# A transformer block on one core: the beginning and the first stacks by halves, row maxima of 512 columns into a scratch tile

## The chip, the cores and the metric

The kernel runs on one core of one Trainium2 chip. The metric is the device time of one execution in microseconds (us), lower is better. The engines are named as the profile names them: PE (TensorE matmul), PEld (its weight loads), DVE (VectorE), ACT (ScalarE), POOL (GpSimd), SP (SyncE, which here only issues DMAs).

## The reference

One pre-norm transformer block in fp32 over T = 2048 tokens of D = 512 (attention that is causal within segments, with a memory between them, then a gated feed-forward part of 1376 columns):

```python
q, k, v = (x @ wq), (x @ wk), (x @ wv)          # 32 heads of 16, 4 segments of 512 tokens
for s in range(4):
    logits = qs @ ks^T * scale + mask           # causal within the segment
    a_dot = softmax(logits) @ vs
    a_mem = phi(qs) @ M / (phi(qs) @ z + 1e-6)  # memory of the segments before
    o = g * a_mem + (1 - g) * a_dot             # g = sigmoid(beta), by head
    M += phi(ks)^T @ vs;  z += sum(phi(ks))
h  = x + A(layernorm(x)) @ wo
h2 = h + (gelu(y @ w_gate) * (y @ w_up)) @ w_down,   y = layernorm(h)
```

## The kernel before

Most products are made from a high and a low part of each operand (`split_weight`, `split_psum`: ACT writes the high part, DVE or POOL subtracts it to get the low one), and three passes: high by high, low by high, high by low. Buffers are 35 rows of SBUF of 512 columns (`row`), 18 slots of two such halves (`slot`), five stacks each for q and k (`stq`, `stk`), and the 8 banks of PSUM (`bank`). A stack holds q or k of some heads, with high, low and high parts taking turns over the partitions; three DMAs (SP, a few on ACT's queue) put each stack together from a slot (`qkv`, L1131 and L1137).

Every operation on every engine is first recorded (`S.op`), and then emitted by `run(order)` in the order of a table of numbers, `ORDER`. The instructions of an engine stand in that order, and a wait is set where an instruction needs another's result or buffer. A buffer is taken from the pool when its operation comes up in the table. So the table sets all of the sequence and the choice of buffers.

The work of the first segment is this. `ln1_first` fetches four tiles of 128 tokens of x, makes their layer norm in two pairs (statistics on DVE L935, first row of a pair normalised on DVE L958, the second on ACT L962), transposes them on PE (L967) and splits them (L972 high, L974 low). Rows of wq, wk and wv are fetched in between (L698, L715) and split (L699 high on ACT, L704 low on POOL, L707 low on DVE). `project_first` (L1026) makes the first q and k for 256 tokens at a time, `vproj` (L1066) v, `qkv` splits q and k (L1118, L1120) and moves them into stacks.

`pass_a` (L1261) computes scores for the row maxima alone: for each of two heads on two partition halves (`a`) and four blocks of 128 tokens (`i`) a product of 128(i+1) columns. One VectorE instruction (L1271) adds the mask, takes the minimum of the negated sum into one column of `nm`, and has to write its elementwise result somewhere, though nobody reads it. For 512 columns (i = 3) that goes back into the bank, for fewer into the tile `aside`, at offsets 0 and 384 in turn (`turns`). `pass_b` (L1319 to L1347) makes the scores again, transposed, with the maxima in them, then exponentials (L1325) and products with v. `sides` (L574) is a small copy from DVE, `tock`, between two groups of products that use both halves of PE.

The feed-forward part follows (L1612, L1780, L1679), and the last results are sums on DVE (L1683) of rows that POOL has added (L1818) to what was put into DRAM earlier (`y_dram`, fetched again at L1817), then outputs (L1687, L1821).

Of the kernel before, what the change touches and what calls it, by code (L numbers as in the profile page):

```python
# [7 lines left out]
F32 = mybir.dt.float32  # L8
# [506 lines left out]
def infini_geglu(ctx: ExitStack, tc: tile.TileContext, x, wq, wk, wv, wo, beta,  # L515
# [8 lines left out]
    def sb(name, shape, dt=F32):  # L524
        return p0.tile(shape, dt, name=name)
# [1401 lines left out]
```

## Time and profile before

| what | value |
|---|---|
| three runs | 724.71, 725.15 (median), 726.09 us |
| the profiled execution's own time | 727.73 us |
| its span | 726.0 us |
| granted TensorE clock, mean | 0.999 |

A row of the timeline has start (us from the start of the span), duration in us, engine, line, operation, output <- input, how many, and in brackets how long the engine had been idle before, and what released it. A row of the table of stretches has the stretch, its length, and the busy time of PE, PEld, DVE, ACT and POOL with their instructions, then PE's granted clock, the DMA engines' busy share and GB/s. In a list of groups stand busy us and the mean ns of one. SPq and ACTq are the queues that issue DMAs.

### The profile page before, as it was taken

How to read it: one execution, taken by the hardware profiler on the slowest of the kernel's cores; microseconds unless marked ns; L12 is line 12 of the kernel's file. 1: busy time of each engine (PE TensorE's matmuls, PEld its weight loads, DVE VectorE, ACT ScalarE, POOL GpSimd, SP SyncE). 2: the span in 40 equal slices, each digit the busy share in tenths (PEclk: the TensorE clock that was granted, in tenths of full speed). 3: DMA queues.
4: the chain of work that ended last, by engine and by line, in shares of the span. 5: the costliest groups of instructions: out<-in, count | busy, mean ns of one | idle time of the engine just before them, and what ended most of it. 6: DMA issues, size and time to landing. Idle time of an engine off the chain costs nothing. (4 is left out here: it accounts for less than half of the span.)

```text
span 726.0 us, 19146 instructions
## 1 busy us (share of the span) xinstructions
PE 709.3 (98%) x6372; PEld 571.4 (79%) x6372; DVE 628.3 (87%) x1992; ACT 529.9 (73%) x1130; POOL 552.8 (76%) x840
## 2 busy tenths in 40 slices
PE   7999999999999999999999999999999999999997
PEld 6888877767878877876867778888888778888885
DVE  6898989978888889999977686889999998789996
ACT  6889888798777877969677577778876866656331
POOL 6454668498846646868897999999999968599936
PEclk9999999999999999999999999999999999999999
DMA  7755557656676776787668465768573047877757
GB/s 261 188 153 170 147 152 185 186 171 188 188 190 171 207 215 190 212 235 213 176 206 266 149 186 184 240 185 256 163 227 124 16 132 215 273 253 242 249 125 252
DMA packets 102646, 140.49 MB, mean 194 GB/s; under 512 B 18468, under 2 KB 40916, under 8 KB 102548
## 3 DMA queue, kind: packets, MB, share of 16 engines
q1 hardware_dynamic: 102388, 139.02, 65.1%
q8 instruction: 50, 0.82, 0.5%
q14 instruction: 48, 0.39, 0.2%
q10 hardware_dynamic: 160, 0.26, 0.2%
HBM read 73.81 MB, written 39.29 MB: 156 GB/s over the span
## 5 line engine op out<-in xcount | busy, mean ns | idle before, releaser
L1325 ACT ACTIVATE row<-bank 128x512 f32<-128x512 f32 x320 | 172.2, 605 | 36.5 <-PE bank L1319 33.8
L1333 POOL TENSOR_SCALAR_AFFINE_SELECT row<-row 128x256 f32<-128x256 f32 (+1 forms) x320 | 109.1, 369 | 75.1 <-ACT row L1325 74.2
L1271 DVE CUSTOM_DVE_ANT_0 aside<-bank,amask 128x256 f32<-128x256 f32 (+2 forms) x384 | 140.6, 418 | 14.4 <-PE bank L1261 4.8
L1005 PE MATMUL bank<-slot,slot 64*128 64x512 f32 x720 | 109.8, 401 | 0.4 <-DVE tock L574 0.4
L1271 DVE CUSTOM_DVE_ANT_0 bank<-bank,amask 128x512 f32<-128x512 f32 x128 | 86.2, 710 | 7.4 <-PE bank L1261 6.9
L1261 PE MATMUL bank<-stk,stq 64*128 64x128 f32 (+3 forms) x512 | 78.7, 327 | 2.2 <-DVE tock L574 1.2
L1005 PEld LDWEIGHTS bank<-slot,slot 64*128 64x128 f32 x720 | 74.7, 185 | 6.5 <-DVE tock L574 0.6
L1319 PE MATMUL bank<-stq,stk 64*128 64x256 f32 (+3 forms) x512 | 78.0, 331 | 0.6 <-DVE nm L1271 0.2
L1347 PE MATMUL bank<-row,vaug 128*32 128x512 f32 (+3 forms) x1024 | 76.6, 435 | 0.9 <-ACT row L1325 0.3
L1791 DVE TENSOR_TENSOR row<-row,bank 128x512 f32<-128x512 f32 x110 | 71.9, 677 | 4.1 <-PE bank L1780 3.1
L1612 PE MATMUL bank<-slot,slot 128*128 128x512 f32 (+1 forms) x282 | 74.3, 391 | 0.0
L1612 PE MATMUL bank<-slot,stk 128*128 128x512 f32 (+1 forms) x249 | 65.9, 390 | 0.1
L1261 PEld LDWEIGHTS bank<-stk,stq 64*128 64x128 f32 x512 | 55.4, 185 | 12.0 <-issue 2.9
L1319 PEld LDWEIGHTS bank<-stq,stk 64*128 64x128 f32 x512 | 54.0, 185 | 11.9 <-DVE nm L1271 3.6
L1612 PEld LDWEIGHTS bank<-slot,slot 128*128 128x128 f32 (+1 forms) x282 | 51.8, 185 | 12.8 <-DVE row L1461 0.4
L1347 PEld LDWEIGHTS bank<-row,vaug 128*32 128x32 f32 x1024 | 31.1, 109 | 34.9 <-issue 32.0
L1612 PEld LDWEIGHTS bank<-slot,stk 128*128 128x128 f32 (+1 forms) x249 | 46.3, 186 | 10.7 <-DVE row L1637 0.5
L1612 PE MATMUL bank<-slot,stq 128*128 128x512 f32 (+1 forms) x195 | 51.5, 390 | 0.0
L1780 PE MATMUL bank<-slot,half 128*128 128x512 f32 x186 | 50.2, 389 | 0.0
L1054 PE MATMUL bank<-slot,slot 64*128 64x256 f32 x672 | 49.9, 284 | 0.2 <-DVE mb L1186 0.2
L1271 DVE DVE_READ_ACCUMULATOR2_ANT nm<- 128x1 f32 x512 | 49.8, 97 | 0.0
L1619 ACT ACTIVATE vaug<-bank 128x512 f32<-128x512 f32 (+1 forms) x66 | 38.7, 594 | 13.2 <-PE bank L1612 12.8
(244 smaller groups left out, 1782.1 us busy)
## 6 DMA issues: line engine op xcount, KB each, us to landing
stq<-slot SPq DMA_DIRECT2D x96, 128.0 KB
stk<-slot SPq DMA_DIRECT2D x94, 128.0 KB
row<-x SPq DMA_DIRECT2D x32, 256.0 KB
pv_dram<-row SPq DMA_DIRECT2D x32, 256.0 KB
row<-r_dram SPq DMA_DIRECT2D x28, 256.0 KB
wd_dram<-half SPq DMA_DIRECT2D x28, 256.0 KB
half<-wd_dram SPq DMA_DIRECT2D x28, 256.0 KB
row<-wu SPq DMA_DIRECT2D x20, 256.0 KB
```

What stands on the lines that cost most here:

```text
L1005: return nc.tensor.matmul(pm[i].t, w[i].t[rows_of(r), wi, dc * P:(dc + 1) * P], XT[s][dc].t[rows_of(r), xi, :], start=(dc, wi, xi, ph) == ...
L1054: return nc.tensor.matmul(pms[n].t[:, 256 * t:256 * t + 256], XT[s][dc].t[rows_of(r), xi, t0:t0 + P], whl[wi].t[rows_of(r), dc // 2, 256 * ...
L1261: nc.tensor.matmul(sa.t[:, c0:c0 + w], sq.t[own, p, i * P:(i + 1) * P], sk.t[own, p, 0:w], start=True, stop=True, tile_position=(64 * a, 0 ...
L1271: nc.vector.tensor_tensor_reduce(out=(sa.t[:, c0:c0 + w] if i > 2 else aside[:, turns[0]:turns[0] + w]), in0=sa.t[:, c0:c0 + w], in1=amask ...
L1319: nc.tensor.matmul(sc.t[:, c0:c0 + D - q0], sk.t[own, p, q0:q0 + P], sq.t[own, p, q0:D], start=True, stop=True, tile_position=(64 * a, 0), ...
L1325: act(w, prio, lambda sc=sc, e=e: nc.scalar.activation(e.t[:, :w], sc.t[:, :w], AF.Exp), [sc, vtab], [e])
L1333: nc.gpsimd.affine_select(v, v, pattern=pat + [[1, P]], compare_op=OP.is_ge, fill=0.0, base=0, channel_multiplier=-1)
L1347: nc.tensor.matmul(pv.t[32 * n:32 * n + 32, kb * P:D], va.t[:, 136 * kb + 17 * j:136 * kb + 17 * j + 32], e.t[:, lo:lo + D - kb * P], star ...
L1612: nc.tensor.matmul(dst.t[:w], v.t[:, wi, c0 + j * w:c0 + (j + 1) * w], b[bk][j].t[:, xi, :], start=first and j == 0 and n == 0, stop=j == ...
L1619: act(D, prio, lambda: nc.scalar.activation(c.t[:w], src.t[:w], AF.Copy), [src], [c])
L1780: nc.tensor.matmul(dst[u].t, ws[a].t[0][:, wi, P * u:P * u + P], h[bk].t[:, xi], start=first and m == 0, stop=m == 2, skip_group_check=True)
L1791: dve(D, prio, lambda u=u, acc=acc: nc.vector.tensor_tensor(acc.t, acc.t, src[u].t, op=OP.add), [src[u]], [acc])
```

## The change

`ln1_first` halves the normalisation of the second row by columns (ACT 0:256, DVE 256:512) and transposes by pairs of column blocks. In `project_first` each of the three passes is an operation of its own. The first stacks (unit `U` = 0, `Q` = 0) are moved by halves of 256 tokens, and the products of 256 columns in `pass_a` need only the first halves (`EARLY`). The maxima of 512 columns write to `aside` too, which grows from 768 to 960 columns, with offsets 0 and 448 in turn. `ORDER` has other numbers throughout. The number of matmuls stays at 5428. Lines of the changed kernel are some 1 to 22 higher: L1026 becomes L1042, L1131 and L1137 become L1154, L1261 L1283, L1271 L1293, L1683 L1705, L1817 L1839, L1687 L1709, L1821 L1843.

```diff
-    aside = sb("aside", [P, 6 * P])
+    aside = sb("aside", [P, 960])
...
 # ln1_first, rows[1]
+                elif h:
                     act(4, prio, lambda t=t: nc.scalar.activation(
                         rows[t].t, rows[t].t, AF.Identity, scale=y.t[:, t:t + 1], bias=b.t[:, t:t + 1]),
...
+                else:
+                    act(4, prio, lambda: nc.scalar.activation(
+                        rows[1].t[:, 0:256], rows[1].t[:, 0:256], AF.Identity, scale=y.t[:, 1:2], bias=b.t[:, 1:2]),
+                        [yh, got], [rows[1], done[0]], src=0.44, acq=[y, b], chain=True)
+                    dve(190, prio, lambda: nc.vector.tensor_scalar(
+                        rows[1].t[:, 256:D], rows[1].t[:, 256:D], mv.t[:, 1, 0:1], y.t[:, 1:2], op0=OP.subtract,
+                        op1=OP.mult), [yh, got], [rows[1], done[1]], acq=[y, mv], chain=True)
...
-            for t in ts:
+            for t in ts if h else []:
...
+            for g in range(2) if h == 0 else []:
+                pe(4 * TR, prio, lambda g=g, pts=pts: [nc.tensor.transpose(
+                    pts[dc].t[:, t * P:t * P + P], rows[t].t[:, dc * P:(dc + 1) * P], ident)
+                    for t in range(2) for dc in (2 * g, 2 * g + 1)], [rows[0], done[g], vident],
+                    pts[2 * g:2 * g + 2], acq=[*dst, rows[1]], chain=True)
...
 # project_first
-                for ks in (((0, 0), (1, 0)), ((0, 1),)):
+                for k, (wi, xi) in enumerate(((0, 0), (1, 0), (0, 1))):
...
 # qkv
-                    if Q == 0 and part == 0:
-                        by_act(prio + 0.2, move, [hl] + zeros, [dst])
+                    for n, (mark, cols) in enumerate(ends if Q == 0 else [([hl], slice(0, D))]):
+                        def move(eng, dst=dst, r=r, part=part, h=h, hl=hl, cols=cols):
+                            eng.dma_start(dst.t[r:P:4, :, cols].bitcast(F32), hl.t[64 * h:64 * h + 64, part, cols].bitcast(F32))
+                        if n == 1 and i == 1 and part == 0:
+                            by_act(prio + 0.2, move, mark[part:part + 1] + zeros, [dst], acq=[hl])
+                        elif Q == 0:
+                            dma(moved + 0.2 + h, lambda move=move: move(nc.sync), mark[part:part + 1] + zeros,
+                                [dst] + [EARLY] * (n == 0),
+                                acq=[hl], kb=85, dur=0.55, chain=True)
...
 # pass_a
-            pe(sum(rr((i + 1) * P) for _, i, _ in cols), prio, f, [sq, sk], sas, acq=[nm],
-               head=0.12, mode="r")
+            pe(sum(rr((i + 1) * P) for _, i, _ in cols), prio, f, soon if cols[0][1] == 1 else [sq, sk],
+               sas, acq=[nm, sq, sk], head=0.12, mode="r")
...
-                        turns[0] = 3 * P - turns[0]
+                        turns[0] = 448 - turns[0]
...
-                            out=(sa.t[:, c0:c0 + w] if i > 2 else aside[:, turns[0]:turns[0] + w]), in0=sa.t[:, c0:c0 + w],
+                            out=aside[:, turns[0]:turns[0] + w], in0=sa.t[:, c0:c0 + w],
...
 # ORDER: one line of it
-    2, 6, 10, 4, 0, 1, 5, 9, 13, 14, 11, 8, 29, 93, 12, 7, 94, 95, 15, 17, 90, 91, 16, 18, 28, 30, 31, 92, 32, 19, 20,
+    80, 4, 6, 103, 0, 1, 5, 11, 12, 10, 9, 13, 8, 30, 14, 91, 92, 97, 98, 15, 17, 16, 19, 18, 20, 94, 95, 96, 99, 7,
```

What the table moves is shown at three places. First the start of the program, the loads on SP's queue and then ACT; SP before:

```order
L925 DMA row2_103<-x 128x512
L925 DMA row3_104<-x 128x512
L925 DMA row4_105<-x 128x512
L698 DMA row5_106<-wk 128x512
L925 DMA row6_107<-x 128x512
L698 DMA row7_108<-wq 128x512
L715 DMA row9_110<-wv 128x512
```

and after, where row0 to row2 and row6 are the four tiles of x:

```order
L928 DMA row0_101<-x 128x512
L928 DMA row1_102<-x 128x512
L928 DMA row2_103<-x 128x512
L699 DMA row3_104<-wq 128x512
L717 DMA row4_105<-wv 128x512
L699 DMA row5_106<-wk 128x512
L928 DMA row6_107<-x 128x512
```

The rows of wq and wv moved ahead of wk, and the fourth tile of x behind all three. ACT's first work, before:

```order
L946 ACTIVATE bank0_65<-bank0_65 128x2 [waits DVE_49]
L699 ACTIVATE slot0_73<-row5_106 128x512 [waits DMAHW3_49]
L962 ACTIVATE row2_103<-row2_103,ln1_163,ln0_162 128x512 [waits DMAHW0_49,DVE_49]
L699 ACTIVATE slot1_74<-row7_108 128x512 [waits DMAHW5_49]
L946 ACTIVATE bank0_65<-bank0_65 128x2 [waits DVE_49]
```

and after (L701 and L720 are the high parts of weights, L970 the half row):

```order
L950 ACTIVATE bank1_66<-bank1_66 128x2 [waits DVE_49]
L701 ACTIVATE slot0_73<-row3_104 128x512 [waits DMAHW3_49]
L720 ACTIVATE slot1_74<-row4_105 128x512 [waits DMAHW4_49]
L970 ACTIVATE row0_101<-row0_101,ln1_163,ln0_162 128x256 [waits DMAHW0_49,DVE_49]
L701 ACTIVATE slot6_79<-row5_106 128x512 [waits DMAHW5_49]
```

One more high part, that of wv, now stands ahead of the normalised half row. The second place is DVE in the maxima of 512 columns near the beginning, before, with the semaphores that a row waits for (the row without a tile on the right reads the accumulator):

```order
L1271 ISA bank3_68,nm0_153<-bank3_68,amask_169 128x512 [waits PE_49]
L1271 ISA nm0_153 128x1
L1271 ISA bank4_69,nm0_153<-bank4_69,amask_169 128x512
L1271 ISA nm0_153 128x1
L911 TENSOR_TENSOR slot14_87<-bank2_67,slot14_87 128x512 [waits Activation_49]
```

and after:

```order
L1293 ISA aside_176,nm1_154<-bank0_65,amask_169 128x512 [waits PE_49]
L1293 ISA nm1_154 128x1
L1293 ISA aside_176,nm1_154<-bank3_68,amask_169 128x512 [waits DVE_49]
L1293 ISA nm1_154 128x1
L764 TENSOR_SCALAR mv0_160<-bn0_158 128x1
```

The second maximum of a pair now waits for DVE itself. The third place is the end of the program on SP, before:

```order
L1817 DMA row31_132<-y_dram_185 128x512
L1687 DMA out_0_dram<-row32_133 128x512
L1817 DMA row5_106<-y_dram_185 128x512
L1817 DMA row28_129<-y_dram_185 128x512
L1821 DMA out_0_dram<-row20_121 128x512
```

and after:

```order
L1839 DMA row18_119<-y_dram_185 128x512
L1839 DMA row4_105<-y_dram_185 128x512
L1839 DMA row0_101<-y_dram_185 128x512
L1709 DMA out_0_dram<-row16_117 128x512
L1843 DMA out_0_dram<-row23_124 128x512
```

The last loads of `y_dram` moved ahead of the first output.

More of the change, by code (lines that the diff above doesn't have):

```diff
@@ L546, in dma, with by_act @@
         return S.op("SP", dur or (0.5 if kb == 256 else 0.7), prio, fn, ins, outs, lat=kb / 255, **k)
-    def by_act(prio, fn, ins, outs):
-        S.op("ACT", 0.45, prio, lambda: fn(nc.scalar), ins, outs, lat=2.4, chain=True)
+    def by_act(prio, fn, ins, outs, acq=()):
+        S.op("ACT", 0.45, prio, lambda: fn(nc.scalar), ins, outs, acq=acq, lat=2.4, chain=True)
     def mm(n):
@@ L698, in split_weight @@
         dma(prio - early, lambda: nc.sync.dma_start(r.t[:rows, :w], src), [], [r], kb=kb, dur=0.5)
+        v.hi = Val()
         act(w, prio, lambda: nc.scalar.activation(v.t[:rows, 0, :w], r.t[:rows, :w], AF.Copy),
-            [r], [v], src=0.092)
+            [r], [v, v.hi], src=0.092)
         r.writers += [q for a in after for q in a.writers]
@@ L923, in ln1_first @@
         rows = [Val(PROW1) for _ in range(4)]
+        got, done = Val(), (Val(), Val())
         for t in range(4):
-            dma(prio - 3 + 0.4 * (t > 1), lambda t=t: nc.sync.dma_start(rows[t].t, x[t * P:t * P + P]), [], [rows[t]],
+            dma(prio - 3 + 0.4 * (t > 1), lambda t=t: nc.sync.dma_start(rows[t].t, x[t * P:t * P + P]), [],
+                [rows[t]] + [got] * (t == 1),
                 kb=170 if t else 300, dur=0.5)
@@ L960, in ln1_first @@
                         [yh, rows[t]], [rows[t]], acq=[y, mv])
-                else:
+                elif h:
                     act(4, prio, lambda t=t: nc.scalar.activation(
@@ L1020, in project_first, with f @@
             cols = slice(256 * h, 256 * h + 256)
+            begun, rest = Val(), Val()
             for dc in range(ND):
-                for ks in (((0, 0), (1, 0)), ((0, 1),)):
-                    def f(dc=dc, ks=ks, pm=pm, cols=cols):
+                for k, (wi, xi) in enumerate(((0, 0), (1, 0), (0, 1))):
+                    def f(dc=dc, wi=wi, xi=xi, pm=pm, cols=cols):
                         for i in range(2):
-                            for wi, xi in ks:
-                                nc.tensor.matmul(pm[i].t[:, 0:256], w[i].t[:, wi, dc * P:(dc + 1) * P],
-                                                 XT[0][dc].t[:, xi, cols], start=(dc, wi, xi) == (0, 0, 0),
-                                                 stop=dc == ND - 1 and xi == 1)
-                    pe(2 * len(ks) * mm(256), prio, f, [*w, XH[h][dc], *(XLH[h][dc:dc + 1] if ks[0][1] else [])], pm,
-                       acq=[XT[0][dc]] + (acq if (h, dc, len(ks)) == (0, 0, 2) else []))
+                            nc.tensor.matmul(pm[i].t[:, 0:256], w[i].t[:, wi, dc * P:(dc + 1) * P],
+                                             XT[0][dc].t[:, xi, cols], start=(dc, wi, xi) == (0, 0, 0),
+                                             stop=dc == ND - 1 and xi == 1, skip_group_check=True)
+                    one_, last = (dc, k) == (0, 0), (dc, k) == (ND - 1, 2)
+                    pe(2 * mm(256), prio, f, [*([v.hi for v in w] if wi == 0 else w), (XLH if xi else XH)[h][dc]]
+                       + ([] if one_ else [begun]) + ([rest] if last else []),
+                       [*pm, *([begun] if one_ else []), *([] if last else [rest])],
+                       acq=[XT[0][dc], *w] + (acq if one_ and h == 0 else []), chain=True)
         return pms
@@ L1090, in vproj @@
                 act(256, prio, g, [pm] + va[k].pre, [va[k]], chain=True)
+    EARLY = Val()
     def qkv(U):
@@ L1114, in qkv @@
             sc = 0.25 if i == 0 else 1.0
+            ends = []
             for pms, cols in parts:
                 pm, n = pms[i], cols.stop - cols.start
-                hi = Val()
+                hi, end = Val(), Val()
+                ends.append(([hi, end], cols))
                 act(n, first, lambda pm=pm, hl=hl, sc=sc, n=n, cols=cols: nc.scalar.activation(
@@ L1121, in qkv @@
                     hl.t[:, 1, cols], pm.t[:, :n], sc, hl.t[:, 0, cols].bitcast(F32), op0=OP.mult, op1=OP.subtract),
-                    [pm, hi], [hl], chain=True)
+                    [pm, hi], [hl, end], chain=True)
                 if r:
@@ L1128, in qkv @@
                 for r, part in enumerate(((0, 1, 0), (0, 0, 1))[i]):
-                    if i == 0:
-                        dma(moved + 0.2 + h, lambda dst=dst, r=r, part=part, h=h, hl=hl:
-                            nc.sync.dma_start(dst.t[r:P:4].bitcast(F32),
-                                              hl.t[64 * h:64 * h + 64, part].bitcast(F32)),
-                            [hl] + zeros, [dst], kb=165, chain=True)
-                        continue
-                    def move(eng, dst=dst, r=r, part=part, h=h, hl=hl):
-                        eng.dma_start(dst.t[r:P:4].bitcast(F32), hl.t[64 * h:64 * h + 64, part].bitcast(F32))
-                    if Q == 0 and part == 0:
-                        by_act(prio + 0.2, move, [hl] + zeros, [dst])
-                    else:
-                        dma(moved + 0.2 + h, lambda move=move: move(nc.sync), [hl] + zeros, [dst], kb=165,
-                            chain=True)
+                    for n, (mark, cols) in enumerate(ends if Q == 0 else [([hl], slice(0, D))]):
[7 more added lines that the diff above has]
+                                acq=[hl], kb=85, dur=0.55, chain=True)
+                        else:
+                            dma(moved + 0.2 + h, lambda move=move: move(nc.sync), mark + zeros, [dst], kb=165,
+                                chain=True)
                 if i == 0 and Q >= len(stq_t):
@@ L1250, in pass_a @@
         sq, sk = STQ[Q], STK[Q]
+        soon = [EARLY] if Q == 0 else [sq, sk]
         def part(cols):
```

541 rows, old and new, of the table ORDER are left out of this document.

## The prediction, as it was put on record before the changed kernel ran

> **What bounds the kernel now.** First the page's head and its list of busy times, then the table of stretches, then the waits of the matrix engine, last the timeline at both ends.
>
> ```profile
> span 726.0 us, 19146 instructions
> PE 709.3 (98%) x6372; PEld 571.4 (79%) x6372; DVE 628.3 (87%) x1992; ACT 529.9 (73%) x1130; POOL 552.8 (76%) x840
> ```
>
> PE is busy for 98% of the span. By stretches (the columns are span, PE, PEld, DVE, ACT, POOL busy, clock, DMA share):
>
> ```profile
> 0.00:5.00 5.00, 0.67 (x4) 0.49 (x5) 1.36 (x3) 1.49 (x2) 2.98 (x15) 1.00 0.58 183
> 20.00:25.00 5.00, 4.32 (x40) 4.00 (x40) 2.89 (x15) 4.99 (x10) 4.78 (x10) 1.00 0.97 281
> 25.00:30.00 5.00, 4.64 (x59) 3.79 (x56) 4.87 (x28) 3.34 (x10) 1.22 (x2) 1.00 0.95 239
> 30.00:40.00 10.00, 9.78 (x131) 8.86 (x129) 9.91 (x37) 9.14 (x23) 2.47 (x9) 1.00 0.50 121
> 100.00:200.00 100.00, 98.91 (x1370) 78.64 (x1362) 89.12 (x392) 82.76 (x185) 74.91 (x144) 1.00 0.68 185
> 200.00:300.00 100.00, 98.69 (x1400) 80.09 (x1400) 86.89 (x370) 78.84 (x175) 56.82 (x131) 1.00 0.74 198
> 400.00:500.00 100.00, 100.00 (x441) 81.26 (x440) 76.45 (x162) 73.70 (x158) 95.20 (x104) 1.00 0.62 195
> ```
>
> From 400 us on PE never idles at full clock (1.00), so an order of the feed-forward part that is merely different gains nothing there. In attention PE loses 1.09 and 1.31 us per 100. At the start 4.33 us go while the first rows of x are fetched, then 0.68, 0.36 and 0.22 between 20 and 40, where VectorE (DVE) is full, 9.91 of 10. So the changeable time is 1.26 us at the start, some 4 in attention (1.2 per 100 over 340), and the tail. PE's longest waits:
>
> ```profile
> PE bank L940 <- POOL ones L634: 4.3, 1, 4.3
> PE bank L1261 <- DVE tock L574: 1.2, 2, 1.0
> PE bank L1261 <- DMA stq<-slot: 0.7, 1, 0.7
> ```
>
> **The beginning by halves.** The timeline of before:
>
> ```profile
> 5.98 0.69 DVE L935 BATCH_NORM_STATS2 bn<-row 128x6 f32<-128x512 f32 x1 [0.48 <-DMA row<-x]
> 6.73 0.63 ACT L699 ACTIVATE slot<-row 128x512 fp32r<-128x512 f32 x1 [1.04 <-DMA row<-wk]
> 7.27 0.80 ACT L962 ACTIVATE row<-row,ln,ln 128x512 f32<-128x512 f32 x1
> 7.44 1.37 POOL L704 TENSOR_TENSOR slot<-row,slot 128x512 fp32r<-128x512 f32 x1 [3.23 <-ACT slot L699]
> 8.08 0.63 ACT L699 ACTIVATE slot<-row 128x512 fp32r<-128x512 f32 x1
> 8.74 0.69 DVE L707 TENSOR_TENSOR slot<-row,slot 128x512 fp32r<-128x512 f32 x1
> 9.22 1.93 PE L1026 MATMUL bank<-slot,slot 128*128 128x256 f32 x10 [0.38 <-ACT slot L972]
> 15.81 0.76 PE L1026 MATMUL bank<-slot,slot 128*128 128x256 f32 x5
> ```
>
> The third load (x) is there at 5.98, the fourth (wk) at 6.73, the sixth (wq) at 8.08: 0.7 us apart. The order of SP's loads after the third changes from wk, x, wq, wv to wq, wv, wk, x. ScalarE (ACT) then takes wq (6.73 to 7.36), wv (fifth load, about 7.4, plus 0.63: 8.1), and only then its half of the second row: half of L962's 0.80, so it ends near 8.5, while L962 ended at 8.07. The split in halves (0.40 saved on ACT, and 0.42 or less more on DVE) is eaten by the wv copy that now stands ahead of it: the first product starts at about 9.6 instead of 9.22. Next, wk's high part comes sixth (8.1, after the half row: 8.5 to 9.2), so its low part on POOL, 1.37, is ready at 10.6 instead of 8.81. On DVE the statistics of the fourth row of x wait for the seventh load (8.8, ends 9.5 with 0.69), and behind them stands the low part of wq (0.69), ready at 10.3 instead of 9.43. PE's third and fourth product wait for these two: two products of about 0.15 (0.76 for five at 15.81) behind 9.6 it is 9.9, so 0.4 for the one, and 0.2 for the other. Against that, third passes are put later, so that PE asks later for the low parts of x. I take +0.6 at the end of the projection (16.57 before), with -0.4 and +1.0 as ends.
>
> **The first stacks by halves.** Six transfers of 128 KB become twelve of 64 KB.
>
> ```profile
> 13.78 0.42 ACT L1118 ACTIVATE slot<-bank 128x256 fp32r<-128x256 f32 x1
> 16.41 5.92 PE L1066 MATMUL bank<-slot,slot 128*128 128x256 f32 x48
> 16.95 0.64 SPq L1131 DMA_DIRECT2D stq<-slot  x1
> 17.22 0.61 ACTq L1137 DMA_DIRECT2D stk<-slot  x1
> 17.90 1.08 ACTq L1137 DMA_DIRECT2D stk<-slot  x1
> 19.04 1.39 SPq L1131 DMA_DIRECT2D stq<-slot  x2
> 23.00 0.73 PE L1261 MATMUL bank<-stk,stq 64*128 64x256 f32 x8 [0.68 <-DMA stq<-slot]
> 23.62 0.42 DVE L1271 CUSTOM_DVE_ANT_0 aside<-bank,amask 128x256 f32<-128x256 f32 x1 [1.20 <-POOL tick L990]
> ```
>
> Before, issues run from 16.95 to 20.4, the last lands at 23.0, and PE had stood for 0.68. After, the first halves leave when the first 256 tokens are done (about 14 us), so the 256-wide scores wait for no transfer: -0.7. The 384 and 512 wide ones need the second halves. Twelve issues instead of six cost 6 x 0.6 more of queue time (SP's and ACT's rows above); the two on ACT (0.61 and 1.08 before) now stand ahead of the last high part of q (L1141), and behind that come DVE's low part and three issues on SP. From the projection's end, 17.2, that is 0.42 for the k half, 1.7 of issues, 0.42 for the q half, as much on DVE, 1.4 of issues, and the 2.6 that lay between 20.4 and 23.0: 24.1. PE is there when the products of L1066 (22.33 before) and the 256-wide scores (0.73) are done: 22.33 + 0.6 + 0.73 = 23.7. So 0.4 is lost again, and the stage nets -0.3 (ends -0.7 and +1.4). DVE starts its maxima about 1 us earlier, but is full from 25 to 40, so a later end of its work there takes the 0.3 back. Both parts of the beginning: +0.6, from -1.0 to +2.0.
>
> **Maxima of 512 columns.** These rows are by line and shape, and from the timeline:
>
> ```profile
> L1271 DVE CUSTOM_DVE_ANT_0 bank<-bank,amask 128x512 f32<-128x512 f32 x128 | 86.2, 710 | 7.4 <-PE bank L1261 6.9
> L1271 DVE CUSTOM_DVE_ANT_0 aside<-bank,amask 128x384 f32<-128x384 f32 x128 | 68.7, 551 | 4.8 <-PE bank L1261 1.6 <-POOL mm L1286 1.4 <-ACT cd L1381 1.0
> 4.33 0.18 DVE L936 BATCH_NORM_AGGREGATE mv<-bn 128x2 f32<-128x6 f32 x1
> 23.97 0.55 DVE L1271 CUSTOM_DVE_ANT_0 aside<-bank,amask 128x384 f32<-128x384 f32 x1
> 24.45 0.08 DVE L1271 DVE_READ_ACCUMULATOR2_ANT nm<- 128x1 f32 x1
> 28.12 0.70 DVE L1271 CUSTOM_DVE_ANT_0 bank<-bank,amask 128x512 f32<-128x512 f32 x1
> 28.74 0.14 DVE L1271 DVE_READ_ACCUMULATOR2_ANT nm<- 128x1 f32 x1
> 28.74 0.73 DVE L1271 CUSTOM_DVE_ANT_0 bank<-bank,amask 128x512 f32<-128x512 f32 x1
> ```
>
> A 384 wide one starts 0.48 before the next, a 512 wide one into the bank 0.62; by the slope of the columns (128 more at 0.133) an aside target would give 0.61. That is 0.01 each, 128 times: 1.3 us of DVE, and the 0.14 reads may fall to 0.08. The other side is a new wait. Aside is 960 columns, and the targets alternate between 0 and 448. A 512 wide one at 0 reaches to 512 and overlaps a neighbour at 448, so it must wait for it. Counted in the program, 93 of the 512 maxima now wait for the instruction right ahead of them; before, none did. The rows show what that costs: without such a wait an instruction starts 0.08 before the end of the one ahead (23.97 against 23.62 + 0.42 = 24.04, 28.74 against 28.82), with it 0.04 after (L935 runs from 3.60 for 0.69, L936 starts at 4.33). So 0.12 each, 93 x 0.12 = 11 us more DVE, 9 to 10 net. What covers it is DVE's idle time: 24.0 us from 100 to 300 (200 less 89.12 and 86.89), of which a share of 200/340 of the waits takes 5.5. PE's loss there is 2.40 us; if it goes as DVE's busy time over its idle time (7.3 before, 181.5/18.5 = 9.8 after), it grows by a third, 0.8, and over 340 us by 1.4. PE waits there for other engines too, so I take two thirds: +0.9. Bounds: nothing (all hidden), and a third of the 11 us, 3.6, if in full stretches such as 30 to 40 every wait goes through.
>
> The Trainium skill (VectorE: DVE Perf Modes, The DRAIN you can't avoid) says that chaining without semaphores gains nothing, since an instruction starts only when the pipe is empty. The rows at 23.97 and 28.74, which start 0.08 before the end, speak against it here. By that rule the term would be 0 and the time 725.35.
>
> **The tail.**
>
> ```profile
> 713.67 0.93 SPq L1817 DMA_DIRECT2D row<-y_dram  x2
> 719.33 2.52 POOL L1818 TENSOR_TENSOR row<-row,row 128x512 f32<-128x512 f32 x2 [1.24 <-DMA row<-y_dram]
> 719.78 0.84 PE L1679 MATMUL bank<-stk,stq 128*128 128x512 f32 x3
> 721.87 0.69 DVE L1683 TENSOR_TENSOR row<-row,bank 128x512 f32<-128x512 f32 x1 [0.54 <-POOL row L1818]
> ```
>
> The last sum on DVE waits 0.54 for POOL, which waits for rows whose loads stood behind an output on SP. Now all five loads stand ahead of the first output. At most 0.54 goes (then PE's end at 720.62 holds DVE); nothing if POOL is late for another reason. I take -0.4.
>
> **The rest of the order.** The number of matmuls is the same. Elsewhere I see no row with a wait of over 1 us that the order removes: 0, within 2 either way (some 4 us of PE idle in attention).
>
> **Sum.** The profiled execution has a span of 726.0 and a time of 727.73, 2.58 over the median 725.15. +0.6 + 0.9 - 0.4 = +1.1: 728.8 by its own measure, 726.25 beside the median, +0.15%. A measurement can tell about 0.2% from no change, 1.45 us: 723.70 to 726.60.
>
> **Rivals.** *Slower:* the own waits come through on a DVE that is already full: +3.6 in place of +0.9, so 728.9. For it speaks 9.91 of 10 at 30 to 40; against it that PE loses only 0.22 there. It decides from 1.25 us on, a ninth of the 11. Chance 0.35. *Faster:* the beginning does what it says. The 0.68 goes, 0.36 and 0.22 too, the tail 0.54, and the own waits hide in DVE's idle time: -1.8, 723.35. For it speaks the wait for stq at 23.00; against it the wv copy ahead of the half row. Chance 0.29. *The change does nothing:* halves land early but a full DVE holds the end of the first maxima: beginning 0, 725.65, a case within 0.2%, and part of the forecast's chance, 0.36.
>
> **How the numbers follow.** Forecast 0.36, slower 0.35, faster 0.29; these are the three chances. The range goes from 723.0 (the faster case with 0.3 more from the order) to 729.6 (the slower one with 0.7 of a late beginning), and leaves out 2 in 10. The forecast's own range is 723.7 to 726.6.
>
> **What would show it.** First product at 9.6 and end of projection near 17.2: beginning right. First scores before 22 with no wait for a transfer, then one for stk or stq of up to 1: the stacks right. Maxima of 512 columns whose next starts 0.73 later, not 0.62, and DVE's busy time or its waits on itself up by some 9 us: own waits right; PE's idle from 100 to 300 at 3.2 instead of 2.4: exposure right. Last sum on DVE within 0.2 of PE's end: tail right. Wrong it would be if PE's idle in attention moved by over 2 us, which the order alone could do.

## The result and the profile after

The changed kernel took 736.04 us (median, 735.06 to 738.01), the kernel before 724.93 in the same job: 1.0151 times as long, 95% interval 1.0137 to 1.0165. That is 11 us slower. 726.25 was forecast, with 729.6 as the upper end.

The head of the page of the changed kernel (its profiled execution took 738.01), then the table of stretches with the columns as above, then PE's and PEld's longest waits:

```profile
span 736.3 us, 19210 instructions
PE 719.0 (98%) x6372; PEld 575.8 (78%) x6372; DVE 633.2 (86%) x1993; ACT 528.8 (72%) x1130; POOL 553.5 (75%) x840
```

```profile
10.00:15.00 5.00, 4.30 (x23) 4.30 (x24) 3.22 (x12) 3.16 (x10) 4.41 (x9) 0.66 0.94 354
20.00:25.00 5.00, 5.00 (x43) 4.73 (x42) 4.09 (x19) 4.28 (x10) 2.65 (x4) 1.00 0.48 114
100.00:200.00 100.00, 97.92 (x1383) 74.80 (x1383) 88.11 (x386) 80.07 (x179) 74.48 (x138) 1.00 0.66 176
200.00:300.00 100.00, 98.44 (x1324) 76.74 (x1323) 86.08 (x360) 77.78 (x171) 55.23 (x127) 1.00 0.70 192
345.00:350.00 5.00, 4.08 (x77) 2.33 (x73) 5.00 (x15) 4.01 (x10) 5.00 (x7) 1.00 0.44 109
350.00:355.00 5.00, 4.71 (x55) 3.12 (x57) 4.38 (x22) 3.50 (x7) 3.47 (x11) 0.74 0.73 166
355.00:360.00 5.00, 4.98 (x56) 3.39 (x56) 4.02 (x21) 3.62 (x10) 4.66 (x8) 0.58 0.47 148
```

```profile
PE bank L944 <- DMA row<-x: 4.3, 1, 4.3
PE bank L1369 <- DVE nm L1293: 1.5, 4, 0.5
PE bank L1341 <- DVE row L1059: 1.2, 1, 1.2
PE bank L1042 <- DVE slot L709: 1.1, 1, 1.1
```

```profile
PEld bank L1283 <- DVE nm L1293: 6.8, 20, 0.6
PEld bank L1341 <- DVE nm L1293: 4.8, 17, 0.4
```

Two things stand out. PE's busy time went from 709.3 to 719.0 for the same 6372 recorded matmuls, so the matmuls got longer, and PE's idle column shows only a small part of the loss (2.08 and 1.56 us per 100 in place of 1.09 and 1.31). The weight loads show more. Before, the two lines of scores waited for maxima like this:

```profile
PEld bank L1319 <- DVE nm L1271: 3.6, 10, 0.5
PEld bank L1261 <- DVE nm L1271: 1.6, 4, 0.6
```

so 14 waits of 5.2 us became 37 of 11.6. The second thing is PE's granted clock: 0.66 from 10 to 15, 0.74 and 0.58 from 350 to 360. Taken by single microseconds it is 0.50 for 3.4 us (from 11.1) and for 6.8 us (from 352.4), so some 5 of the 9.7 us of longer matmuls are these falls. They are not the main loss: another execution of the changed kernel, at a mean clock of 0.999, took 735.06.

The row maxima, in the timeline:

```profile
34.50 0.68 DVE L1293 CUSTOM_DVE_ANT_0 aside<-bank,amask 128x512 f32<-128x512 f32 x1
35.10 0.08 DVE L1293 DVE_READ_ACCUMULATOR2_ANT nm<- 128x1 f32 x1
35.22 0.69 DVE L1293 CUSTOM_DVE_ANT_0 aside<-bank,amask 128x512 f32<-128x512 f32 x1
35.84 0.08 DVE L1293 DVE_READ_ACCUMULATOR2_ANT nm<- 128x1 f32 x1
```

The second starts 0.72 after the first, 0.04 behind the end of the read of the accumulator, where the pair of before stood 0.62 apart and overlapped. This one waits for VectorE alone. Another pair shows a maximum that waits for PE as well:

```profile
30.65 0.68 DVE L1293 CUSTOM_DVE_ANT_0 aside<-bank,amask 128x512 f32<-128x512 f32 x1
31.26 0.09 DVE L1293 DVE_READ_ACCUMULATOR2_ANT nm<- 128x1 f32 x1
31.49 0.69 DVE L1293 CUSTOM_DVE_ANT_0 aside<-bank,amask 128x512 f32<-128x512 f32 x1
```

It starts 0.84 after the first, 0.14 behind the end of the read. Counted in the program, 39 of the 93 maxima wait for VectorE alone and 54 for another engine too (a semaphore instruction then stands ahead of the maximum). In the trace the median start is 0.035 behind the read for the 39 and 0.144 for the 54. A maximum with such a second wait, but none for the instruction right ahead, starts 0.08 before the end of the read, like the others. So a wait costs 0.12 in 39 places and 0.23 in 54, which makes 16.9 us of VectorE. Of 88 maxima of 512 columns with another maximum behind them the median distance is 0.83 and the shortest 0.61; 28 lie between 0.72 and 0.74, 42 between 0.83 and 0.88. Before, the median was 0.62.

Measured against before by the count of products, the lag grows as follows in the profiled executions: 2.3 us at the end of the projection (1.7 of it the fall of the clock), up to some 4 in the first third of the `pass_a` products, 8 at 90% of them, 11.7 at the last product of L1634 in the feed-forward part, 10.3 at the end of the span.

### The profile page after: what moved, and what is told of

Its sections match the earlier page's. It is cut to its first block, busy times and chain, and to the rows that moved or that the text cites. A ratio compares the mean times of both kernels' runs of the same rounds, so it can differ in the third digit from the quotient of the medians.

```text
span 736.3 us, 19210 instructions
## 1 busy us (share of the span) xinstructions
PE 719.0 (98%) x6372; PEld 575.8 (78%) x6372; DVE 633.2 (86%) x1993; ACT 528.8 (72%) x1130; POOL 553.5 (75%) x840
## 4 chain that ended last, share of the span: by engine, by line
PE 86%; DVE 9%; issue 2%; ACT 1%; DMA 1%; SPq 0%; DVEq 0%; ACTq 0%
PE bank L1634 29%; PE bank L1802 12%; PE bank L1021 9%; PE bank L1369 8%; DVE aside L1293 6%; PE bank L1073 5%; PE bank L1283 5%; PE bank L1341 5%; PE bank L1442 3%; PE bank L1701 3%; PE bank L1449 2%; PE bank L1250 2%; PE bank L1042 1%; PE bank L1085 1%; DMA row<-x 1%
## 5 line engine op out<-in xcount | busy, mean ns | idle before, releaser
L1293 DVE CUSTOM_DVE_ANT_0 aside<-bank,amask 128x128 f32<-128x128 f32 (+3 forms) x512 | 227.7, 487 | 26.2 <-PE bank L1283 10.3
L1634 PE MATMUL bank<-slot,slot 128*128 128x512 f32 (+1 forms) x330 | 87.1, 390 | 0.0
L1341 PE MATMUL bank<-stq,stk 64*128 64x256 f32 (+3 forms) x512 | 83.9, 337 | 1.4 <-DVE row L1059 1.2
L1283 PE MATMUL bank<-stk,stq 64*128 64x128 f32 (+3 forms) x512 | 81.6, 335 | 1.7 <-DVE nm L1293 1.0
L1021 PEld LDWEIGHTS bank<-slot,slot 64*128 64x128 f32 x720 | 73.8, 185 | 6.5 <-issue 0.4
L1634 PEld LDWEIGHTS bank<-slot,slot 128*128 128x128 f32 (+1 forms) x330 | 61.2, 186 | 14.1 <-issue 0.4
L1802 PE MATMUL bank<-slot,half 128*128 128x512 f32 x276 | 71.8, 390 | 0.0
L1599 POOL TENSOR_TENSOR slot<-row,slot 128x512 fp32r<-128x512 f32 (+3 forms) x55 | 61.3, 1118 | 8.9 <-ACT slot L1597 8.9
L1283 PEld LDWEIGHTS bank<-stk,stq 64*128 64x128 f32 x512 | 55.5, 187 | 15.4 <-DVE nm L1293 6.8
L1802 PEld LDWEIGHTS bank<-slot,half 128*128 128x128 f32 x276 | 51.7, 188 | 11.0 <-DVE row L1664 0.3
L1073 PEld LDWEIGHTS bank<-slot,slot 64*128 64x128 f32 x672 | 45.7, 186 | 1.3 <-ACT row L1057 0.4
L1783 POOL TENSOR_TENSOR slot<-row,slot 128x512 fp32r<-128x512 f32 x31 | 40.0, 1297 | 6.2 <-ACT slot L1781 6.0
L1634 PE MATMUL bank<-slot,stq 128*128 128x512 f32 (+1 forms) x162 | 43.7, 390 | 0.0
```

Source lines behind the costliest of these rows:

```text
L1021: return nc.tensor.matmul(pm[i].t, w[i].t[rows_of(r), wi, dc * P:(dc + 1) * P], XT[s][dc].t[rows_of(r), xi, :], start=(dc, wi, xi, ph) == ...
L1073: return nc.tensor.matmul(pms[n].t[:, 256 * t:256 * t + 256], XT[s][dc].t[rows_of(r), xi, t0:t0 + P], whl[wi].t[rows_of(r), dc // 2, 256 * ...
L1283: nc.tensor.matmul(sa.t[:, c0:c0 + w], sq.t[own, p, i * P:(i + 1) * P], sk.t[own, p, 0:w], start=True, stop=True, tile_position=(64 * a, 0 ...
L1293: nc.vector.tensor_tensor_reduce(out=aside[:, turns[0]:turns[0] + w], in0=sa.t[:, c0:c0 + w], in1=amask[:, D - w:], op0=OP.add, op1=OP.min ...
L1341: nc.tensor.matmul(sc.t[:, c0:c0 + D - q0], sk.t[own, p, q0:q0 + P], sq.t[own, p, q0:D], start=True, stop=True, tile_position=(64 * a, 0), ...
L1599: pool(0.14 + 2.13e-3 * (hi - lo), prio, lambda: nc.gpsimd.tensor_tensor(v.t[:, 1, :hi - lo], r.t[:, lo:hi], v.t[:, 0, :hi - lo].bitcast(F ...
```

## The experiments

Ratios are to the kernel before in the same job. W is the theory that the waits of VectorE on itself cost the time, O that the new order does.

**1. The waits taken away in the changed kernel.** With 1024 columns no neighbours overlap; only a 16-bit tile of that size fits.

```diff
-    aside = sb("aside", [P, 960])
+    aside = sb("aside", [P, 1024], mybir.dt.bfloat16)
-                        turns[0] = 448 - turns[0]
+                        turns[0] = 512 - turns[0]
```

> The changed kernel, with the scratch tile in 16-bit floats, 1024 columns, offsets 0 and 512: neighbours never overlap, so of the 93 maxima that wait for the instruction right ahead on VectorE one is left. The elementwise result that nobody reads is rounded. Theory W (the waits of VectorE on itself make the attention part longer): 736 comes down by 5 to 8 us, to 728 to 731, and the lag behind before grows by under 2 us between 40 and 340 us of the span, where it grows from 2.5 to 8 now. Rival O (the new order is worse in attention whatever the waits): within 1.5 us of 736.

726.19 us, 1.0008 (0.9995 to 1.0022): 9.9 us less than the changed kernel (10.4 by the two ratios), more than was expected, and all but 0.5 of its loss. In the profiled executions the lag behind before is 0.6 at the end of the projection and, by the count of `pass_a` products, between +0.6 and -4.5 through the attention; the steady growth is gone. W holds.

**2. The waits alone, in the order of before.** The kernel before with `aside` of 960 columns, offsets 0 and 448, and all maxima into it: 89 waits for the instruction right ahead.

```diff
-    aside = sb("aside", [P, 6 * P])
+    aside = sb("aside", [P, 960])
-                        turns[0] = 3 * P - turns[0]
+                        turns[0] = 448 - turns[0]
-                            out=(sa.t[:, c0:c0 + w] if i > 2 else aside[:, turns[0]:turns[0] + w]), ...
+                            out=aside[:, turns[0]:turns[0] + w], ...
```

> The kernel before, its order untouched, with the maxima of 512 columns into the scratch tile of 960 columns at offsets 0 and 448: 89 maxima wait for the instruction right ahead, none did. Theory W: 4 to 7 us slower than before, 729 to 732, in attention. Rival O: within 1.5 us of before.

735.11 us, 1.0124 (1.0109 to 1.0140), 9.4 us slower at the medians, more than the 4 to 7 that were expected. Without any other part of the change, the waits make nearly the same loss. The head of its page has the same sign as the changed kernel's, at a clock of 0.999, and the weight loads show where:

```profile
PE 714.7 (97%) x6372; PEld 571.2 (78%) x6372; DVE 631.1 (86%) x1992; ACT 530.0 (72%) x1130; POOL 552.9 (75%) x840
```

```profile
PEld bank L1319 <- DVE nm L1271: 5.2, 14, 0.5
PEld bank L1261 <- DVE nm L1271: 4.2, 12, 0.8
```

With the same matmuls in the same order, the span is 7.8 us longer: PE's busy time by 5.4, its idle time by only 2.4. Of the 89 waits 31 are for VectorE alone and 58 for another engine too, by the prices above 16.8 us of VectorE; 9.4 of them came through, 56%.

**3. wq's low part early.** One number of `ORDER`: L709 (93) stands ahead of the statistics of the fourth tile of x (29) on VectorE; their load (7) is on SP.

```diff
-    ... 96, 99, 7, 29, 93, 31, ...
+    ... 96, 99, 93, 7, 29, 31, ...
```

> The changed kernel, with the low part of wq (DVE L709) put ahead of the statistics of the fourth tile of x, two rows earlier on VectorE. Theory C (L709 took 1.38 instead of 0.69 because POOL's subtraction ran at the same time, PE stood 1.1 for it, and its clock fell to about 0.65 for 4 us): L709 runs from about 7.8 to 8.5 in 0.69, PE waits under 0.4, the clock from 10 to 15 is above 0.9, the projection ends 1.8 to 2.6 earlier, and the whole is 2 to 2.5 us faster, about 733.7. Rival G (given back, since VectorE is full from 25 to 40): the projection ends earlier, the whole stays within 0.8 us of 736.

735.17 us, 1.0138 (1.0119 to 1.0157), 0.9 less than the changed kernel's median in its own job: inside the spread of the two. What the edit does is visible in the rows. In the changed kernel, POOL and VectorE ran two subtractions of two rows in SBUF each at the same time, and PE stood for the second:

```profile
8.82 1.27 POOL L706 TENSOR_TENSOR slot<-row,slot 128x512 fp32r<-128x512 f32 x1 [4.82 <-ACT slot L701]
9.27 1.38 DVE L709 TENSOR_TENSOR slot<-row,slot 128x512 fp32r<-128x512 f32 x1
10.06 1.73 POOL L722 TENSOR_TENSOR slot<-row,slot 128x512 fp32r<-128x512 f32 x1
10.70 2.65 PE L1042 MATMUL bank<-slot,slot 128*128 128x256 f32 x12 [1.12 <-DVE slot L709]
```

and in this experiment these two ran apart, VectorE's in half the time:

```profile
7.24 0.69 DVE L709 TENSOR_TENSOR slot<-row,slot 128x512 fp32r<-128x512 f32 x1
9.13 1.28 POOL L706 TENSOR_TENSOR slot<-row,slot 128x512 fp32r<-128x512 f32 x1 [5.14 <-ACT slot L701]
10.37 1.30 POOL L722 TENSOR_TENSOR slot<-row,slot 128x512 fp32r<-128x512 f32 x1
10.40 1.55 DVE L962 TENSOR_SCALAR row<-row,mv,ln 128x512 f32<-128x512 f32 x1
10.47 1.58 PE L1042 MATMUL bank<-slot,slot 128*128 128x256 f32 x11 [0.46 <-POOL slot L706]
```

But PE now waits 0.46 for POOL's L706, and the next POOL subtraction meets another VectorE row (L962, 1.55 instead of 0.54). The projection ends 1.7 us earlier than in the changed kernel's profiled execution (16.91 against 18.62 for the start of its last product), and the clock there is 1.00. The edit is not what makes that: in experiment 1, where L709 collides as in the changed kernel (1.37), but the clock does not fall, the last product starts at 16.91 too. So the 1.7 are the fall (3.4 us at half clock).

**4. The wait filled.** Five more small transposes on PE while it waits for L709, ahead of the first product with a low part.

```diff
+                        if (h, dc, wi) == (0, 0, 1):
+                            for _ in range(5):
+                                nc.tensor.transpose(WARM[0].t[0:24, 0:P], ident[:, 0:24], ident)
```

`WARM[0]` is the bank to which the small transposes at the start of the program write.

> The changed kernel, with five small transposes more on PE (results unread) in the 1.1 us in which it waits for L709. The wait stays, PE does not stand idle in it. If the clock fell because PE stood idle: the clock from 10 to 15 is above 0.9 and the whole 1.2 to 1.8 us faster. If it fell for another reason: 0.66 as now, and within 0.5 us of 736.

736.17 us, 1.0143 (1.0124 to 1.0162): no gain that can be told. The clock from 10 to 15 is 1.00 in its profile, as it would be if the idle PE were the reason, but it is 1.00 in experiment 1 too, where nothing was filled in. So the clock falls there in some executions only, and this experiment doesn't settle why.

**5. Half of the waits.** As 2, but the maxima of p = 1 go to the bank: 40 waits.

```diff
-                            out=aside[:, turns[0]:turns[0] + w], ...
+                            out=(sa.t[:, c0:c0 + w] if i > 2 and p == 1 else aside[:, turns[0]:turns[0] + w]), ...
```

> The kernel before with the scratch tile of 960 columns, but of the maxima of 512 columns only those of the first head of a pass write to it, the others to the bank as before: 40 maxima wait for the instruction right ahead instead of 89. Theory L (VectorE and PE hand work to each other in a loop without slack, each wait of 0.12 comes through): in proportion, 40/89 of the 9.4 us, +4.2, from 3 to 5. Rival T (a threshold: VectorE's idle time hides the first waits): under +2.

729.61 us, 1.0058 (1.0046 to 1.0070), 4.2 us slower, as the proportion said. No threshold shows: 40 waits cost 0.105 us each, 89 cost 0.106 each. By the prices above the 40 (15 for VectorE alone, 25 for another engine too) are 7.5 us of VectorE, and 56% came through, as in experiment 2.

**6. The same dose the other way.** The kernel before, with maxima of 512 columns over 400 of them (the input and the mask are cut alike).

```diff
+                        u = 400 if i > 2 else w
-                            out=(sa.t[:, c0:c0 + w] if i > 2 ...
+                            out=(sa.t[:, c0:c0 + u] if i > 2 ...
```

> The kernel before, but the maxima of 512 columns look at 400 of them (112 left out, all of them or their diagonal part), so that each of 128 takes about 0.12 less, 15 us of VectorE in all: the same dose as the waits, with the other sign. Theory L: 6 to 14 us faster than before, 712 to 720. Rival S (one-sided: PE is the bound once VectorE keeps up): under 3 us faster.

722.75 us, 0.9958 (0.9944 to 0.9971): 2.7 faster at the medians, where 15 us of VectorE were taken away. What is added comes through by just over half, what is taken away by a fifth. Rival S holds on this side.

**7. The target alone.** The kernel before with the tile of experiment 1.

```diff
-    aside = sb("aside", [P, 6 * P])
+    aside = sb("aside", [P, 1024], mybir.dt.bfloat16)
-                        turns[0] = 3 * P - turns[0]
+                        turns[0] = 512 - turns[0]
-                            out=(sa.t[:, c0:c0 + w] if i > 2 else aside[:, turns[0]:turns[0] + w]), ...
+                            out=aside[:, turns[0]:turns[0] + w], ...
```

> The kernel before, its order untouched, all maxima into a scratch tile of 1024 columns of 16-bit floats at offsets 0 and 512: no maximum waits for the instruction right ahead. If the target itself (scratch instead of bank) matters: over 1 us faster or slower than before. Theory W: within 1 us (128 times 0.01 to 0.04 less VectorE), so that all of the 9.4 us of the scratch tile of 960 columns is the waits.

724.94 us, 0.9991 (0.9981 to 1.0001). Writing to this scratch tile instead of the bank is worth 0.5 us at the medians, 1.4 at the end of the interval, and it is no loss; the loss of experiment 2 is the waits.

**8. Three edits to the changed kernel.** No overlaps (experiment 1), wq's low part early (experiment 3), and one layer-norm row (L844, number 3099 in `ORDER`) 26 numbers later, behind the next two maxima of 512 columns.

```diff
-    ... 3134, 3099, 2827, 2828, ... 2767, 2766, 2804, ...
+    ... 3134, 2827, 2828, ... 2767, 2766, 3099, 2804, ...
```

In the changed kernel that row collided with POOL too:

```profile
347.42 1.29 POOL L1408 TENSOR_TENSOR row<-row,row 128x512 f32<-128x512 f32 x1
347.47 1.52 DVE L844 TENSOR_SCALAR row<-row,mv,ln 128x512 f32<-128x512 f32 x1
349.51 0.67 DVE L1059 SCALAR_TENSOR_TENSOR row<-bank,row 128x512 f32<-128x512 f32 x1
350.24 0.84 PE L1341 MATMUL bank<-stq,stk 64*128 64x384 f32 x6 [1.16 <-DVE row L1059]
```

Such a row takes 0.53 alone. PE stood 1.16 for what came behind it, and 2.1 us later its clock fell to 0.50 for 6.8 us (the stretches above: 5 x 0.26 + 5 x 0.42 = 3.4 us of full clock).

> The changed kernel with three edits: the scratch tile of 1024 columns without overlaps; the low part of wq (L709) ahead of the statistics of the fourth tile; and one layer-norm row (L844) put some rows later on VectorE, where POOL has no sum of two rows at the same time (it took 1.5 instead of 0.53, PE stood 1.0 for it, and its clock was 0.5 to 0.67 for the next 7 us). If PE's falls of clock come from such waits: the clock stays above 0.97 from 300 to 400 in the profile, and the time is 1.5 to 3.5 us under the 726.2 of the first experiment, so under before by 1 to 3. Rival (other waits take their place): 725.5 to 727.

723.28 us, 0.9964 (0.9952 to 0.9976): 2.1 us under before in the same job, the fastest of the versions that compute everything. The clock from 300 to 400 is 1.00, and the row and the L1059 that stood behind it, and now stands ahead of it, read:

```profile
337.04 0.68 DVE L1059 SCALAR_TENSOR_TENSOR row<-bank,row 128x512 f32<-128x512 f32 x1
339.33 0.66 DVE L844 TENSOR_SCALAR row<-row,mv,ln 128x512 f32<-128x512 f32 x1
```

**9. VectorE's time without waits.** The kernel before with 64 copies of 96 columns on VectorE, ahead of the second maximum of each pair of 512.

```diff
+                        if i > 2 and a == 1:
+                            nc.vector.tensor_copy(junk[:, 96 * p:96 * p + 96], amask[:, 0:96])
```

`junk` is a new tile of 192 columns.

> The kernel before with 64 short copies more on VectorE (96 columns, results unread), one ahead of the second maximum of 512 columns of each pair, none of them waiting for VectorE itself. Each takes about 0.1 to 0.12. If what the waits cost is VectorE's time in that place (theory D): 64 times 0.1 to 0.12 times the 0.9 that came through of the waits, 5.5 to 7 us slower. If a wait on itself costs something else (theory E): under 3 us slower.

734.64 us, 1.0115 (1.0096 to 1.0134), 8.9 slower: VectorE's time in that place costs without any wait on itself. The dose was larger than planned, as the list of groups by shape shows:

```profile
L1273 DVE COPY junk<-amask 128x96 f32<-128x96 f32 x64 | 21.4, 334 | 0.0
```

0.33 us on average (0.21 at the median, 1.33 at most; the 25 that took longer than 0.21 all ran beside an instruction of POOL). Less the overlap of 0.08 some 16 us were added, and 55% of them came through. By the prices above that is the same share as of the waits, so theory D holds, with just over a half in place of the 0.9.

**10. Waits and shorter maxima together.** Experiment 2 with 400 of 512 columns, offsets 0 and 390, so that the same 89 wait.

```diff
-                        turns[0] = 448 - turns[0]
+                        turns[0] = 390 - turns[0]
+                        u = 400 if i > 2 else w
-                            out=aside[:, turns[0]:turns[0] + w], ...
+                            out=aside[:, turns[0]:turns[0] + u], ...
```

> The kernel before with the same 89 waits as in the second experiment (scratch tile of 960 columns, offsets 0 and 390), but the maxima of 512 columns look at 400 of them (112 left out), each 0.12 shorter, which is more than the waits add (15 us against 10.4). Theory D: the waits are paid for by the shorter maxima, within 2 us of before. Theory E: the 9.4 us of the waits on top of the 722.7 of the shorter maxima, 730 to 733.

727.08 us, 1.0016 (1.0004 to 1.0027), 1.4 slower: theory D. The waits add 16.8 us by the prices above, not the 10.4 of the expectation, and the shorter maxima take 15 away, so VectorE has some 2 us more to do than before.

**11. Without wq's edit.** Experiment 8 without the early wq (the `+` line of experiment 3 taken back).

> The changed kernel without overlaps in the scratch tile (as in the first experiment) and with the layer-norm row (L844) later, but wq's low part where the change put it. If the row's collision with POOL and PE's fall of clock behind it make most of the 2.9 us between the first experiment and the one with three edits: 723.3 to 724.5. If the beginning makes it: 725.3 to 726.5.

725.37 us, 0.9986 (0.9968 to 1.0004): just inside the second forecast, but by the ratios halfway between experiments 8 and 1, and its interval reaches into both of theirs. Of its twelve executions five lie from 722.8 to 723.7, where those of experiment 8 are (722.4 to 723.7), and seven from 725.2 to 727.8. With L709 colliding, PE waits 1.0 there in the profile (an execution of 723.44, without a fall of the clock behind the wait). So what each of the two edits has of the 2.9 us isn't settled.

**12. The maxima undone.** The changed kernel's order with both moves, the maxima of 512 columns to the bank and the tile of 768 columns as before the change.

```diff
-                            out=aside[:, turns[0]:turns[0] + w], ...
+                            out=(sa.t[:, c0:c0 + w] if i > 2 else aside[:, turns[0]:turns[0] + w]), ...
```

> The changed kernel with the maxima of 512 columns undone (they write to the bank, the scratch tile has 768 columns and offsets 0 and 384 again), wq's low part early and the layer-norm row later. No maximum waits for the instruction right ahead. If the target does not matter (the seventh experiment): 722.5 to 724.5, like the version with three edits, 1 to 3 us under before. If the 16-bit scratch tile gave part of that version's gain: 724.5 or more.

725.38 us, 0.9998 (0.9982 to 1.0014): not the gain of experiment 8. Either the scratch tile without overlaps is worth something in this order, unlike in experiment 7, or other waits make the difference: in the profiled execution (726.73) PE waits 1.9 for a DMA that isn't late in experiment 8.

```profile
PE bank L1283 <- DMA row<-wv: 1.9, 1, 1.9
```

Whether that wait belongs to the edit, and which of the two it is, stays open.

VectorE's time added or taken against the time (waits at 0.12 for VectorE alone and 0.23 with another engine: 31 and 58 in experiments 2 and 10, 15 and 25 in experiment 5; 128 maxima shorter by 0.12; copies as measured):

| experiment | VectorE, us (estimate) | ratio to before | time, us |
|---|---|---|---|
| 6, shorter maxima | -15 | 0.9958 | -2.7 |
| 10, waits and shorter maxima | +2 | 1.0016 | +1.4 |
| 5, 40 waits | +7.5 | 1.0058 | +4.2 |
| 9, 64 copies | +16 | 1.0115 | +8.9 |
| 2, 89 waits | +16.8 | 1.0124 | +9.4 |

## Why the prediction was wrong

**The step that failed is the exposure of the own waits, and with it their price.** Their number (93) was right. The price of 0.12 holds for the 39 that wait for VectorE alone (0.73 against 0.61 from one start to the next). The 54 that wait for another engine too cost 0.23, so the term "93 x 0.12 = 11" is 16.9 us. The larger failure is "what covers it is DVE's idle time". From the 11 us +0.9 was taken, a twelfth; as a rival, a third was given, 3.6 us. In experiment 2, 9.4 of 16.8 us came through, just over half, as in experiments 5 and 9, and experiment 1 gives 9.9 for the 93. Half of the 11 us would already have been 5.5, above the rival; the prediction's twelfth of the right 16.9 would have been 1.4.

The reasoning took VectorE's 24 idle us from 100 to 300 as slack, and PE's 2.40 us of idle there as all that PE loses to VectorE. Both readings were wrong. VectorE's idle time there was not used up (25.8 us after, by 88.11 and 86.08), since the stage grew with the waits: most of it is time in which VectorE waits for a product that PE hadn't made yet. And PE's wait for a maximum shows mostly as longer matmuls and as waits of the weight loads, not as idle PE (experiment 2: 5.4 us busy, 2.4 idle). That also spoils the sign that was named for the exposure: PE's idle from 100 to 300 was to be 3.2 if it was right, and came out at 3.64, near it, while the time missed by 10 us. Experiment 5 loses as much per wait with 40 waits as experiment 2 with 89, so no slack showed.

That the removal of VectorE's time pays only by a fifth (experiment 6) fits a kernel that stood, before, near where the two engines balance. Whether PE's own work is what then holds, instruction by instruction, was not tried.

**By the rule of the Trainium skill** (VectorE: DVE Perf Modes, The DRAIN you can't avoid) that a semaphore between chained instructions costs nothing extra, the waits would have cost nothing. The same section adds that a next instruction which is not held starts earlier; the prediction left that out, and the rows at 23.97 and 28.74 do start earlier. The runs decide: 89 waits cost 9.4 us.

**The beginning.** The first product came at 9.08 instead of 9.6; with the same beginning it came at 9.30 in experiment 1 and at 10.38 in experiment 4, so half a microsecond is within what executions differ there. wq's low part was ready at 10.65, 10.3 had been said, so near, but for another reason: not the statistics ahead of it, but 0.69 us more of its own, by the collision with POOL that the prediction missed. PE's wait of 0.4 became 1.12, in this execution with a fall of the clock behind it. In experiment 1, with the same beginning and no fall, it was 0.45, and the last product of the projection starts 0.6 later than before (16.91 against 16.29), as forecast, though with L709 at twice its time that was in part luck. The total of +0.6 held to within what can be told: with the waits gone, the rest of the change is worth 1.0008.

**The stacks.** Right that the first scores wait for no transfer: PE's 0.68 from 20 to 25 is gone, 5.00 of 5. They start at 23.15, not before 22, in the execution with the fall of the clock, and at 21.44 in experiment 1. The second wait, 0.4, did not come.

**The tail.** The last rows of the changed kernel's timeline (of the three sums on DVE the last starts at 731.74):

```profile
730.38 2.05 DVE L1705 TENSOR_TENSOR row<-row,bank 128x512 f32<-128x512 f32 x3 [1.35 <-PE bank L1701]
730.79 0.84 PE L1701 MATMUL bank<-slot,slot 128*128 128x512 f32 x3
```

Right in what moved: the last sum on DVE starts 0.1 behind PE's end and no longer waits for POOL. From PE's last product to the end of the span it is 736.3 - 731.6 = 4.7 us, where it was 726.0 - 720.6 = 5.4: -0.7, where -0.4 had been taken and 0.54 given as the most. Where the rest comes from was not looked at.

**The order elsewhere.** It was set to 0 within 2. Experiment 1 agrees at the median, and experiment 8 shows that one row was badly placed: +1 of wait, and in some executions a fall of the clock. (That PE never idles from 400 us on was read from one stretch; before, it was busy for 99.88 of 100 from 500 to 600.)

## What to carry to other kernels

When a scratch target is shared by neighbours, check whether the ranges of consecutive instructions overlap, or each will wait for the one ahead: here 0.12 us each, and 0.23 where the instruction waits for another engine as well. Take the price from both kinds of rows. Idle time of the second busiest engine wasn't slack here, where it and PE hand work back and forth; a small experiment that adds a known dose in that place, and one that takes it away, tells what comes through. And a planner's table has to know which instructions of VectorE and POOL slow each other.

## What the runs showed of the hardware

Subtractions of two rows in SBUF on VectorE took 1.38 us instead of 0.69 with POOL's running beside them, and a layer-norm row 1.52 instead of 0.53. In these rows the instruction that started first kept its time (POOL's L706 1.27 and L1408 1.29, against 1.28 in experiment 3 and 1.29 in experiment 8), and the one that started while it ran took longer, POOL's too (L722, begun beside L709: 1.73 against 1.30). The Trainium skill (GPSIMD Engine Reference, Specifications) says that the two share their SBUF interfaces, with contention where VectorE has two SBUF inputs or a 2-port mode; the subtractions have two such inputs and agree, the mode of the layer-norm rows doesn't show in the trace, and the prediction had not looked for it.

PE's granted clock fell to 0.50, for 3.4 or 6.8 us, behind single waits of 1.0 to 1.2 us, in some executions and not in others. It did so twice in the changed kernel's profile (0.4 us behind the wait of 1.12, 2.1 us behind the one of 1.16) and once in experiment 1's (behind a wait of 1.0 for L1059). Nothing fell behind the 1.2 for the same row in experiments 3 and 4, the 1.0 for L709 in experiment 11 or the 1.9 in experiment 12. Executions of experiment 1 took 723.7 to 725.4 us at a mean clock of 1.000, and 729.7 at 0.990. The Trainium skill (TensorE: Matmul & The Clock Gate, HAM oscillation) speaks of idle gaps of more than about 3.4 us; here waits a third as long stood ahead of the falls. That the wait has a part in the fall is suggested by the order of the two, but not shown: the filled wait (experiment 4) could not tell.
